# Six instead of four whole-array f-tiles at the head of block 0, taken row tile by row tile of x

## The chip, the cores and the metric

The kernel runs on one core of a Trainium2 chip. The metric is the device time of one execution in microseconds (us), lower is better. All engines of the core run side by side[...]: PE (TensorE, with its weight loads listed apart as PEld), DVE (VectorE), ACT (ScalarE), POOL (GpSimd) and SP (SyncE, which here only issues DMAs).

## What is computed

A two-layer block with a squared ReLU between the layers. x is 2048 x 576, w1 576 x 4608, w2 4608 x 576, all bf16.

```python
h = jnp.einsum("bsd,df->bsf", x, w1) + b1
r = jnp.where(h > zero, h, zero)
h = r * r
out = jnp.einsum("bsf,fd->bsd", h, w2) + b2
```

## The kernel before

**Tiles.** The 2048 rows of x are four blocks of 512 (SB); a block is four row tiles of 128 (RT). The 4608 columns of w1 are 36 f-tiles of 128 (NFT). The contraction over 576 is four chunks of 128 rows (NC) and a rest of 64. Phase A makes the transposed hidden layer hT, 128 f x 512 rows per f-tile and block; phase B (L311 to L338) multiplies it with w2.

**The usual step of phase A.** `a_step(b, j)` (L216) makes the two f-tiles of pair j with 18 matmuls of 64 contraction rows each, nine for each f-tile, in `a_part` (L208, matmul L213). One f-tile uses the upper 64 rows of the PE array and the other the lower 64, so two matmuls run side by side. Its weights lie in `w1h`, which is cut into nine pieces of 64 rows for that purpose, and it needs the transposed block xT in both halves of the partitions; `place` (L201) says where a piece lies. `evac_h` (L195) then takes each f-tile out of PSUM: ScalarE adds b1 and applies the ReLU (L197), VectorE squares (L199).

**The head of block 0.** Blocks 1 to 3 get xT by a transposing DMA (`load_xT`, L263). That would be late for block 0, so block 0 loads x as it is (`load_x`, L91), transposes it on PE into PSUM (`transpose_chunks`, L177, matmul L182) and copies the result to xT on VectorE or ScalarE (`copy_psum`, L171: L175 on VectorE, L173 on ScalarE, and L187). While `w1h` is still on its way, the first G = 4 f-tiles (two pairs) are made another way, with the whole array: `load_quad` (L94) brings 128 rows of w1 by 4 x 128 columns, and `full_mm(half, c)` (L225, matmul L228) multiplies chunk c by half a block, 256 columns at a time, into four PSUM banks bk0. The rest of 64 contraction rows is added from `qr` at L254. Three copies on VectorE (L256 to L258) then fill the second halves of xT, the four banks are evacuated (L259), and `a_step(0, 2)` to `a_step(0, 17)` follow (L292). In blocks 1 to 3 all 18 pairs go through `a_step`, those of the head last (L298).

**The order of the work.** It is written by hand: each engine runs its instructions as the program lists them. The order at the head before the change is

```python
    transpose_chunks(0, (0,), (V,))
    transpose_chunks(0, (1,), (A,))
    transpose_chunks(0, (2,), (A,))
    transpose_chunks(0, (NC,), (V,))
    full_mm(0, 0)
    transpose_chunks(0, (3,), (A,))
    full_mm(0, 1)
    full_mm(0, 2)
    transpose_chunks(1, (0, 1), (V, A))
    full_mm(0, 3)
```

and so on (L240 to L255). One half of a block is two row tiles of x, so a transposed chunk needs two of the four loads of x.

**Queues and buffers.** Eight loads are issued at the opening barrier (`issue_at_barrier`, L126, moves them there), four on SP's queue (x row tile 0, w1 chunks 0 and 2, x row tile 3) and four on ScalarE's (x row tile 1, w1 chunk 1, x row tile 2, w1 chunk 3). After the barrier SP issues the two rests (L104) and then the pieces of `w1h` (L99), pair 2 first. The DMAs use eight semaphores in turn, so that each waits for the one eight before it. Five warm-up matmuls on constant data (L169) run on PE from the barrier on. PSUM has eight banks of 128 x 512 fp32, all in one pool.

Of the kernel before, what the change touches and what calls it, by code (L numbers as in the profile page):

```python
# [11 lines left out]
BF16 = mybir.dt.bfloat16  # L12
# [5 lines left out]
def kernel(  # L18
# [9 lines left out]
    nc = tc.nc  # L28
    P = 128
    H = 64  # L30
    x2 = x.flatten_outer_dims()
    out2 = out.flatten_outer_dims()
    S, D = x2.shape
    F = w1.shape[1]
    FH = F // 2
    G = 4
    NFT = F // P
    NJ = NFT // 2
    NC = D // P
    NH = D // H  # L40
    DM = NC * P
    SB = 512
    NSB = S // SB
    RT = SB // P
    HALF = SB // 2
# [9 lines left out]
    psum = ctx.enter_context(tc.tile_pool(name="psum", bufs=8, space=PSUM))  # L55

    def bank(name):
        return psum.tile([P, SB], FP32, name=name, tag="bank")
# [10 lines left out]
    def early(n):  # L69
        at[0] += n  # L70
        assert at[0] <= NFT * D
        return w2_sb[:, at[0] - n:at[0]]


    xT = [early(XW).rearrange("p (w s) -> p w s", s=SB) for b in range(NSB - 1)]
    xT3 = xpool.tile([P, NH, SB], BF16, name="xT3", tag="xT3")
    xT.append(xT3[:])
    xs = early(RT * D).rearrange("p (j c) -> p j c", c=D)
    qn = early(NC * 4 * P).rearrange("p (c f) -> p c f", c=NC)
    qr = early(2 * P)  # L80
    pairs = [(0, 2), (1, 3)] + [(f, f + G) for f in range(G, NFT) if (f // G) % 2]
    slot = {ft: (h, j) for j, pr in enumerate(pairs) for h, ft in enumerate(pr)}
    assert len(pairs) == NJ and len(slot) == NFT

# [6 lines left out]
    def load_x(eng, j):  # L91
        eng.dma_start(out=xs[:, j, :], in_=x_view[:, j, :])

    def load_quad(eng, c):  # L94
        eng.dma_start(out=qn[:, c, :], in_=w1[c * P:(c + 1) * P, 0:G * P])

    def load_w1(eng, h, j0, n, cs):
        f0 = pairs[j0][h] * P
        eng.dma_start(out=w1h[h * H:(h + 1) * H, cs, j0 * P:(j0 + n) * P], in_=w1_rows[:, cs, f0:f0 + n * P])  # L99
# [1 line left out]
    NWARM = 5  # L101

    def load_rest(eng, h):
        eng.dma_start(out=qr[h * H:(h + 1) * H, :], in_=w1[DM:D, 2 * h * P:2 * (h + 1) * P])  # L104

    b1T = const.tile([P, NFT], FP32, name="b1T")
    warm = const.tile([P, 1], FP32, name="warm")
    load_x(nc.sync, 0)
    load_x(nc.scalar, 1)
    load_quad(nc.sync, 0)  # L110
    load_quad(nc.scalar, 1)
    load_quad(nc.sync, 2)
    load_x(nc.scalar, 2)
    load_x(nc.sync, 3)
    load_quad(nc.scalar, 3)
    nc.scalar.activation(out=warm[:], in_=nc.const_aps.tensor(1.0, [P, 1], FP32), func=ACT.Relu)
    for h in range(2):
        load_rest(nc.sync, h)


    for j0, n in ((2, 1), (3, 1), (4, 1), (5, 1), (6, 1), (7, 1), (8, 2), (10, 2), (12, 2), (14, 4)):
        for h in range(2):
            load_w1(nc.sync, h, j0, n, slice(0, NH))


    def issue_at_barrier(nc):  # L126
        entry, body = nc.main_func.blocks[:2]
        for engine in (mybir.EngineType.SP, mybir.EngineType.Activation):
            mine = [i for i in body.instructions if i.engine == engine and not isinstance(i, mybir.InstNoOp)]
            n = 0  # L130
            while isinstance(mine[n], mybir.InstDMACopy) and not mine[n].has_wait():
                n += 1
            assert n >= 3
            at = next(k for k, i in enumerate(entry.instructions)
                      if i.engine == engine and isinstance(i, mybir.InstEventSemaphore))
            for k, i in enumerate(mine[:n]):
                body.instructions.remove(i)
                entry.instructions.insert(at + k, i)

    nc.at_finalize(issue_at_barrier)  # L140


# [17 lines left out]
    ident = const.tile([P, P], BF16, name="ident")  # L160
# [10 lines left out]
    def copy_psum(eng, dst, src):  # L171
        if eng is nc.scalar:
            nc.scalar.copy(out=dst, in_=src)  # L173
        else:
            nc.vector.tensor_copy(out=dst, in_=src)  # L175

    def transpose_chunks(half, cs, engs):  # L177
        tps = [psum.tile([P, HALF], BF16, name="tp", tag="bank") for c in cs]
        for i in range(2):
            for c, tp in zip(cs, tps):  # L180
                d0 = c * P if c < NC else D - P
                nc.tensor.transpose(tp[:, i * P:(i + 1) * P], xs[:, 2 * half + i, d0:d0 + P], ident[:])  # L182
        cols = slice(half * HALF, (half + 1) * HALF)
        for c, tp, eng in zip(cs, tps, engs):
            copy_psum(eng, xT[0][:, c if c < NC else 7, cols], tp[:])
            if c == NC:
                nc.vector.tensor_copy(out=xT[0][0:H, 8, cols], in_=tp[H:P, :])  # L187

    def hT_of(b, ft):
        if b < NSB - 1:  # L190
            return hT[b][:, ft, :].rearrange("p (j s) -> p j s", j=RT)
        h, j = slot[ft]
        return w1h[:, h * RT:(h + 1) * RT, j * P:(j + 1) * P]

    def evac_h(b, ft, bk):  # L195
        r = rpool.tile([P, SB], BF16, name="r", tag="r")
        nc.scalar.activation(out=r[:], in_=bk[:], func=ACT.Relu, bias=b1T[:, ft:ft + 1], scale=1.0)  # L197
        r3 = r[:].rearrange("p (j s) -> p j s", j=RT)
        nc.vector.tensor_tensor(out=hT_of(b, ft), in0=r3, in1=r3, op=ALU.mult)  # L199

    def place(hi, c):  # L201
        if hi:
            return c // 2 if c % 2 else (3 + c // 2 if c else 8)
        return 8 if c == 8 else (4 if c % 2 else 0) + c // 2
# [11 lines left out]
    def a_step(b, j):  # L216
        bk = [bank("ph") for _ in range(2)]
        a_part(b, j, bk, range(NH))
        for h in range(2):
            evac_h(b, pairs[j][h], bk[h])  # L220


    bk0 = [bank("ph") for _ in range(G)]

    def full_mm(half, c):  # L225
        cols = slice(half * HALF, (half + 1) * HALF)
        for q in range(4):
            nc.tensor.matmul(bk0[q][:, cols], lhsT=qn[:, c, q * P:(q + 1) * P], rhs=xT[0][:, c, cols],  # L228
                             start=(half == 0 and c == 0), stop=False, skip_group_check=True)

    V, A = nc.vector, nc.scalar
    transpose_chunks(0, (0,), (V,))
    transpose_chunks(0, (1,), (A,))
    transpose_chunks(0, (2,), (A,))
    transpose_chunks(0, (NC,), (V,))
    full_mm(0, 0)
    transpose_chunks(0, (3,), (A,))
    full_mm(0, 1)
    full_mm(0, 2)
    transpose_chunks(1, (0, 1), (V, A))  # L240
    full_mm(0, 3)
    transpose_chunks(1, (2, NC), (A, V))
    full_mm(1, 0)
    transpose_chunks(1, (3,), (V,))
    full_mm(1, 1)
    b1T_ps = psum.tile([P, P], BF16, name="b1T_ps", tag="bank")
    nc.tensor.transpose(b1T_ps[:], b1_rows[:], ident[:])  # L247
    nc.vector.tensor_copy(out=b1T[:], in_=b1T_ps[:, 0:NFT])
    full_mm(1, 2)
    full_mm(1, 3)  # L250
    for i in range(2):
        for h in range(2):
            rows = slice(h * H, (h + 1) * H)
            nc.tensor.matmul(bk0[2 * h + i][:], lhsT=qr[rows, i * P:(i + 1) * P], rhs=xT[0][rows, place(h, 8), :],  # L254
                             start=False, stop=True, skip_group_check=True)  # L255
    nc.vector.tensor_copy(out=xT[0][0:H, 4:7, :], in_=xT[0][H:P, 0:3, :])  # L256
    nc.vector.tensor_copy(out=xT[0][H:P, 4:7, :], in_=xT[0][0:H, 1:4, :])
    nc.vector.tensor_copy(out=xT[0][H:P, 8, :], in_=xT[0][0:H, 0, :])  # L258
    for q in range(G):  # L259
        evac_h(0, q, bk0[q])  # L260


    def load_xT(b):  # L263
# [3 lines left out]

    load_xT(1)
    for h in range(2):
        load_w1(nc.sync, h, 0, 2, slice(0, NH))  # L270
    for b in range(2, NSB):
        load_xT(b)
    w2_view = w2_dram.rearrange("(ft p) d -> p ft d", p=P)
# [2 lines left out]
    def load_w2(c, n=1):  # L276
        nc.sync.dma_start(out=w2_sb[:, c * W2CH * D:(c + n) * W2CH * D].rearrange("p (ft d) -> p ft d", d=D),
                          in_=w2_view[:, c * W2CH:(c + n) * W2CH, :])
# [9 lines left out]
    def finish_xT(b):  # L288
        nc.vector.tensor_copy(out=xT[b][0:H, 8, :], in_=xT[b][H:P, 7, :])
        nc.vector.tensor_copy(out=xT[b][H:P, 8, :], in_=xT[b][0:H, 0, :])  # L290

    for j in range(2, NJ):  # L292
        a_step(0, j)
        if j == NJ - 2:
            finish_xT(1)
    load_w2(0)
    for b in range(1, NSB):
        for j in (*range(2, NJ), 0, 1):  # L298
            a_step(b, j)
            if j == NJ // 2 and b + 1 < NSB:  # L300
                finish_xT(b + 1)
        if b == 1:
            load_w2(1)
        if b == 2:
            load_w2(2, 2)
# [5 lines left out]
    for pr in range(NSB // 2):  # L311
        pc = bank("pc")
        for ft in range(NFT):
            for h in range(2):
                nc.tensor.matmul(pc[h * H:(h + 1) * H, :], lhsT=w2(ft, DM, D), rhs=hT_of(2 * pr + h, ft),  # L315
                                 start=(ft == 0), stop=(ft == NFT - 1))
# [52 lines left out]
```

## Time and profile before

| what | before |
|---|---|
| three runs | 289.96, 290.08, 290.81 us (median 290.08) |
| the profiled execution | 290.45 us, of it span 288.7 us |
| PE busy | 284.9 us (99%) |
| weight loads (PEld) busy | 133.7 us (46%) |
| DVE, ACT busy | 79.5 us (28%), 95.6 us (33%) |
| granted TensorE clock in the span | 1.00 |
| HBM read, written | 11.94 MB, 2.36 MB |

The span runs from the first to the last instruction of the profiled execution; 1.75 us of that execution's own time lie around it. In the profile's groups, a line gives source line, engine, operation, output and input tiles by name, shape, count, then busy time and mean ns of one, then the idle time of the engine just before, with what ended it. `w_sb` in the names stands for the large weight buffer: at the head of the kernel it holds x, xT, the chunks of w1 and their rest, since w2 arrives later. Matmuls are pipelined, so a matmul's recorded length (273 ns for 256 columns) is longer than the distance to the next one; what counts for the time is the distance. The chain of waits leads back from the last instruction, at each step to what released it; its pieces are given in order of time as start, length, what.

### The profile page before, as it was taken

Reading aid. Unit: us, or ns where it says so; the run is one execution under the profiler, and the core shown is the slowest. Engines: PE = TensorE matmul, PEld = TensorE weight load, DVE = VectorE, ACT = ScalarE, POOL = GpSimd, SP = SyncE. Lnnn points to the kernel's source line nnn. Section 1 sums busy time; section 2 is a strip of 40 time slices with the busy share of each in tenths; the row PEclk is TensorE's granted clock in tenths of the full one; section 3 lists DMA queues with packets and bytes.
Section 4 is the critical chain, followed back from the end, with each engine's and each line's share of the span. In section 5 each row is a group of like instructions: output and inputs, shape, how many; then the busy total and the mean of one; then the engine's idle time right before and its main releaser. Section 6 shows DMA issues by size and latency. Waiting matters only on the chain.

```text
span 288.7 us, 4818 instructions
## 1 busy us (share of the span) xinstructions
PE 284.9 (99%) x2067; PEld 133.7 (46%) x2078; DVE 79.5 (28%) x196; ACT 95.6 (33%) x153; POOL 1.5 (1%) x8
## 2 busy tenths in 40 slices
PE   9999999999999999999999999999999999999996
PEld 5544444444444444444445444444444444444454
DVE  1644454444445444444420011111100111111111
ACT  3666666766666676666620000000000000000000
POOL 2000000000000000000000000000000000000000
PEclk9999999999999999999999999999999999999999
DMA  7999999910400004300000100000000000000000
GB/s 200 205 190 204 172 185 208 321 50 2 122 3 0 3 2 142 106 0 2 0 2 19 20 20 20 20 23 5 15 20 23 20 20 20 23 20 22 20 23 20
DMA packets 35381, 18.01 MB, mean 62 GB/s; under 512 B 21652, under 2 KB 35360, under 8 KB 35360
## 3 DMA queue, kind: packets, MB, share of 16 engines
q1 hardware_dynamic: 34752, 17.14, 26.4%
q10 hardware_dynamic: 576, 0.56, 0.6%
q8 instruction: 16, 0.26, 0.4%
q14 instruction: 5, 0.04, 0.0%
q0 software_dynamic: 32, 0.01, 0.0%
HBM read 11.94 MB, written 2.36 MB: 50 GB/s over the span
## 4 chain that ended last, share of the span: by engine, by line
PE 98%; DMA 1%; issue 0%; DVE 0%; ACTq 0%
PE ph L213 47%; PE po L329 43%; PE pc L315 5%; PE ph L228 2%; DMA w_sb<-in_x_dram 1%; PE tp L182 1%; PE ph L254 0%; DVE o_sb L331 0%; PE b1T_ps L247 0%; ACTq L353 0%
## 5 line engine op out<-in xcount | busy, mean ns | idle before, releaser
L197 ACT ACTIVATE r<-ph,b1T 128x512 bf16<-128x512 f32 x144 | 91.0, 685 | 48.4 <-PE ph L213 46.4
L213 PE MATMUL ph<-w_sb,w1h 64*128 64x512 bf16 x936 | 101.2, 376 | 0.0
L213 PEld LDWEIGHTS <-w1h 64*128 64x128 bf16 x1260 | 61.3, 94 | 74.6
L329 PE MATMUL po<-w_sb,hT 128*128 128x512 bf16 x423 | 92.9, 379 | 0.5
L329 PEld LDWEIGHTS <-hT 128*128 128x128 bf16 x432 | 42.2, 98 | 51.2 <-issue 0.4
L199 DVE TENSOR_TENSOR hT<-r 128x512 bf16<-128x512 bf16 x108 | 46.0, 426 | 54.7 <-ACT r L197 54.2
L331 DVE TENSOR_TENSOR o_sb<-po,b_bc 128x512 bf16<-128x512 f32 (+2 forms) x17 | 11.2, 660 | 116.7 <-PE po L329 109.7
L213 PE MATMUL ph<-xT,w1h 64*128 64x512 bf16 x324 | 35.1, 376 | 0.0
L329 PE MATMUL po<-w_sb,w1h 128*128 128x512 bf16 (+2 forms) x178 | 31.2, 336 | 0.1
L329 PEld LDWEIGHTS <-w1h 128*128 128x128 bf16 x180 | 16.2, 98 | 15.3
L199 DVE TENSOR_TENSOR w1h<-r 128x512 bf16<-128x512 bf16 x36 | 15.3, 426 | 19.6 <-ACT r L197 19.5
L315 PE MATMUL pc<-hT,w_sb 128*64 128x512 bf16 x108 | 15.7, 379 | 0.0
L315 PEld LDWEIGHTS <-w_sb 128*64 128x64 bf16 x144 | 8.1, 110 | 7.6 <-issue 0.4
L315 PE MATMUL pc<-w1h,w_sb 128*64 128x512 bf16 x36 | 7.9, 379 | 0.0
L317 ACT ACTIVATE oc<-pc,b2T 128x512 bf16<-128x512 f32 x2 | 1.4, 687 | 13.7 <-PE pc L315 13.7
L325 DVE COPY o_sb<-oc 128x64 bf16<-128x64 bf16 x16 | 2.8, 172 | 9.3 <-DMA oc<-oc 9.3
L228 PE MATMUL ph<-w_sb 128*128 128x256 bf16 x32 | 5.3, 313 | 0.0
L228 PEld LDWEIGHTS <-w_sb 128*128 128x128 bf16 x32 | 3.4, 115 | 0.6
L175 DVE COPY w_sb<-tp 128x256 bf16<-128x256 bf16 x5 | 1.5, 292 | 5.9 <-PE tp L182 5.9
L182 PE MATMUL tp<-ident,w_sb 128*128 128x128 bf16 x20 | 2.7, 264 | 0.1
L169 PE MATMUL wps<-one 128*128 128x512 bf16 x5 | 2.3, 628 | 0.4 <-DVE one L144 0.4
L182 PEld LDWEIGHTS <-w_sb 128*128 128x128 bf16 x20 | 1.9, 118 | 1.4 <-DMA w_sb<-in_x_dram 1.2
(27 smaller groups left out, 10.7 us busy)
## 6 DMA issues: line engine op xcount, KB each, us to landing
w_sb<-in_w_dram SPq DMA_DIRECT2D x2, 1728.0 KB, 8.7
w1h<-in_w_dram SPq DMA_DIRECT2D x8, 288.0 KB, 5.9
out_dram<-o_sb SPq DMA_DIRECT2D x15, 144.0 KB, 1.8
w1h<-in_w_dram SPq DMA_DIRECT2D x12, 144.0 KB, 3.7
w_sb<-in_w_dram SPq DMA_DIRECT2D x2, 864.0 KB, 7.2
w1h<-in_w_dram SPq DMA_DIRECT2D x2, 576.0 KB, 11.2
w_sb<-in_x_dram SPq DMA_DIRECT2D x2, 144.0 KB, 3.4
w_sb<-in_x_dram ACTq DMA_DIRECT2D x2, 144.0 KB, 3.5
```

The source lines that it names most:

```text
L169: nc.tensor.matmul(wps[:], lhsT=ones[:, 0:P], rhs=ones[:], start=(i == 0), stop=(i == NWARM - 1))
L175: nc.vector.tensor_copy(out=dst, in_=src)
L182: nc.tensor.transpose(tp[:, i * P:(i + 1) * P], xs[:, 2 * half + i, d0:d0 + P], ident[:])
L197: nc.scalar.activation(out=r[:], in_=bk[:], func=ACT.Relu, bias=b1T[:, ft:ft + 1], scale=1.0)
L199: nc.vector.tensor_tensor(out=hT_of(b, ft), in0=r3, in1=r3, op=ALU.mult)
L213: nc.tensor.matmul(bk[h][:], lhsT=w1h[rows, c, j * P:(j + 1) * P], rhs=xT[b][rows, place(h, c), :], start=(i == 0), stop=(i == NH - 1))
L228: nc.tensor.matmul(bk0[q][:, cols], lhsT=qn[:, c, q * P:(q + 1) * P], rhs=xT[0][:, c, cols], start=(half == 0 and c == 0), stop=False, ski ...
L315: nc.tensor.matmul(pc[h * H:(h + 1) * H, :], lhsT=w2(ft, DM, D), rhs=hT_of(2 * pr + h, ft), start=(ft == 0), stop=(ft == NFT - 1))
L317: nc.scalar.activation(out=oc[:, pr, :], in_=pc[:], func=ACT.Identity, bias=b2T[:], scale=1.0)
L325: nc.vector.tensor_copy(out=o_sb[:, DM:D], in_=o_tr[pr][:, jj, h * H:(h + 1) * H])
L329: nc.tensor.matmul(po[:, 0:e - a], lhsT=hT_of(b, ft)[:, jj, :], rhs=w2(ft, a, e), start=(ft == 0), stop=(ft == NFT - 1))
L331: nc.vector.tensor_tensor(out=o_sb[:, a:e], in0=po[:, 0:e - a], in1=b2_bc[:, a:e], op=ALU.add)
```

## The change

G becomes 6, so three pairs instead of two are made with the whole array in block 0, and `a_step(0, j)` begins with j = 3. The pairs are formed anew: (0, 3), (1, 4), (2, 5), and then (6 + i, 21 + i). The loads are regrouped: all four row tiles of x on SP's queue, all four chunks of w1, now 128 x 768, on ScalarE's, all eight at the barrier. The transposes are made row tile by row tile: `transpose_tile(j, c, n, eng)` transposes n chunks of row tile j into one PSUM tile and copies them with one instruction on one engine (with two for the rest). `full_mm(j, n, c)` multiplies chunk c by n row tiles from j on, so by 128, 256 or 512 columns, for six f-tiles. The order of these calls is new. `w1h` is loaded from pair 3 on, and pairs 0 to 2 are loaded later with 384 columns at a time where 0 and 1 came with 256. The copies L256 to L258, the evacuation, phase B and the loads of w2 are as before.

```diff
     S, D = x2.shape
     F = w1.shape[1]
     FH = F // 2
-    G = 4
+    G = 6
+    GP = G // 2
     NFT = F // P
     NJ = NFT // 2
     NC = D // P
...
     xT3 = xpool.tile([P, NH, SB], BF16, name="xT3", tag="xT3")
     xT.append(xT3[:])
     xs = early(RT * D).rearrange("p (j c) -> p j c", c=D)
-    qn = early(NC * 4 * P).rearrange("p (c f) -> p c f", c=NC)
-    qr = early(2 * P)
-    pairs = [(0, 2), (1, 3)] + [(f, f + G) for f in range(G, NFT) if (f // G) % 2]
+    qn = early(NC * G * P).rearrange("p (c f) -> p c f", c=NC)
+    qr = early(GP * P)
+    pairs = [(i, GP + i) for i in range(GP)] + [(G + i, G + NJ - GP + i) for i in range(NJ - GP)]
     slot = {ft: (h, j) for j, pr in enumerate(pairs) for h, ft in enumerate(pr)}
     assert len(pairs) == NJ and len(slot) == NFT
 
...
     NWARM = 5
 
     def load_rest(eng, h):
-        eng.dma_start(out=qr[h * H:(h + 1) * H, :], in_=w1[DM:D, 2 * h * P:2 * (h + 1) * P])
+        eng.dma_start(out=qr[h * H:(h + 1) * H, :], in_=w1[DM:D, GP * h * P:GP * (h + 1) * P])
 
     b1T = const.tile([P, NFT], FP32, name="b1T")
     warm = const.tile([P, 1], FP32, name="warm")
-    load_x(nc.sync, 0)
-    load_x(nc.scalar, 1)
-    load_quad(nc.sync, 0)
-    load_quad(nc.scalar, 1)
-    load_quad(nc.sync, 2)
-    load_x(nc.scalar, 2)
-    load_x(nc.sync, 3)
-    load_quad(nc.scalar, 3)
+    for j in range(RT):
+        load_x(nc.sync, j)
+        load_quad(nc.scalar, j)
     nc.scalar.activation(out=warm[:], in_=nc.const_aps.tensor(1.0, [P, 1], FP32), func=ACT.Relu)
     for h in range(2):
         load_rest(nc.sync, h)
 
 
-    for j0, n in ((2, 1), (3, 1), (4, 1), (5, 1), (6, 1), (7, 1), (8, 2), (10, 2), (12, 2), (14, 4)):
+    for j0, n in ((3, 1), (4, 1), (5, 1), (6, 1), (7, 1), (8, 1), (9, 1), (10, 2), (12, 2), (14, 4)):
         for h in range(2):
             load_w1(nc.sync, h, j0, n, slice(0, NH))
 
...
             n = 0
             while isinstance(mine[n], mybir.InstDMACopy) and not mine[n].has_wait():
                 n += 1
-            assert n >= 3
+            assert n >= RT
             at = next(k for k, i in enumerate(entry.instructions)
                       if i.engine == engine and isinstance(i, mybir.InstEventSemaphore))
             for k, i in enumerate(mine[:n]):
...
         else:
             nc.vector.tensor_copy(out=dst, in_=src)
 
-    def transpose_chunks(half, cs, engs):
-        tps = [psum.tile([P, HALF], BF16, name="tp", tag="bank") for c in cs]
-        for i in range(2):
-            for c, tp in zip(cs, tps):
-                d0 = c * P if c < NC else D - P
-                nc.tensor.transpose(tp[:, i * P:(i + 1) * P], xs[:, 2 * half + i, d0:d0 + P], ident[:])
-        cols = slice(half * HALF, (half + 1) * HALF)
-        for c, tp, eng in zip(cs, tps, engs):
-            copy_psum(eng, xT[0][:, c if c < NC else 7, cols], tp[:])
-            if c == NC:
-                nc.vector.tensor_copy(out=xT[0][0:H, 8, cols], in_=tp[H:P, :])
+    def transpose_tile(j, c, n, eng):
+        cols = slice(j * P, (j + 1) * P)
+        tp = psum.tile([P, n, P], BF16, name="tp", tag="bank")
+        for k in range(n):
+            d0 = (c + k) * P if c < NC else D - P
+            nc.tensor.transpose(tp[:, k, :], xs[:, j, d0:d0 + P], ident[:])
+        c0 = c if c < NC else 7
+        copy_psum(eng, xT[0][:, c0:c0 + n, cols], tp[:])
+        if c == NC:
+            copy_psum(eng, xT[0][0:H, 8, cols], tp[H:P, 0, :])
 
     def hT_of(b, ft):
         if b < NSB - 1:
...
             evac_h(b, pairs[j][h], bk[h])
 
 
+    V, A = nc.vector, nc.scalar
+    transpose_tile(0, 0, 2, V)
+    transpose_tile(0, 2, 2, A)
+    transpose_tile(0, NC, 1, V)
     bk0 = [bank("ph") for _ in range(G)]
 
-    def full_mm(half, c):
-        cols = slice(half * HALF, (half + 1) * HALF)
-        for q in range(4):
+    def full_mm(j, n, c):
+        cols = slice(j * P, (j + n) * P)
+        for q in range(G):
             nc.tensor.matmul(bk0[q][:, cols], lhsT=qn[:, c, q * P:(q + 1) * P], rhs=xT[0][:, c, cols],
-                             start=(half == 0 and c == 0), stop=False, skip_group_check=True)
-
-    V, A = nc.vector, nc.scalar
-    transpose_chunks(0, (0,), (V,))
-    transpose_chunks(0, (1,), (A,))
-    transpose_chunks(0, (2,), (A,))
-    transpose_chunks(0, (NC,), (V,))
-    full_mm(0, 0)
-    transpose_chunks(0, (3,), (A,))
-    full_mm(0, 1)
-    full_mm(0, 2)
-    transpose_chunks(1, (0, 1), (V, A))
-    full_mm(0, 3)
-    transpose_chunks(1, (2, NC), (A, V))
-    full_mm(1, 0)
-    transpose_chunks(1, (3,), (V,))
-    full_mm(1, 1)
+                             start=(j == 0 and c == 0), stop=False, skip_group_check=True)
+
+    full_mm(0, 1, 0)
+    transpose_tile(1, 0, 2, V)
+    transpose_tile(1, 2, 2, A)
+    full_mm(1, 1, 0)
+    full_mm(0, 2, 1)
+    transpose_tile(1, NC, 1, V)
+    transpose_tile(2, 0, 2, A)
+    full_mm(2, 1, 0)
+    transpose_tile(2, 2, 2, V)
+    full_mm(2, 1, 1)
+    full_mm(0, 2, 2)
+    transpose_tile(2, NC, 1, A)
+    transpose_tile(3, 0, 2, V)
+    full_mm(3, 1, 0)
+    transpose_tile(3, 2, 2, A)
+    full_mm(3, 1, 1)
+    transpose_tile(3, NC, 1, V)
+    full_mm(2, 2, 2)
     b1T_ps = psum.tile([P, P], BF16, name="b1T_ps", tag="bank")
     nc.tensor.transpose(b1T_ps[:], b1_rows[:], ident[:])
     nc.vector.tensor_copy(out=b1T[:], in_=b1T_ps[:, 0:NFT])
-    full_mm(1, 2)
-    full_mm(1, 3)
-    for i in range(2):
+    full_mm(0, RT, 3)
+    for i in range(GP):
         for h in range(2):
             rows = slice(h * H, (h + 1) * H)
-            nc.tensor.matmul(bk0[2 * h + i][:], lhsT=qr[rows, i * P:(i + 1) * P], rhs=xT[0][rows, place(h, 8), :],
+            nc.tensor.matmul(bk0[GP * h + i][:], lhsT=qr[rows, i * P:(i + 1) * P], rhs=xT[0][rows, place(h, 8), :],
                              start=False, stop=True, skip_group_check=True)
     nc.vector.tensor_copy(out=xT[0][0:H, 4:7, :], in_=xT[0][H:P, 0:3, :])
     nc.vector.tensor_copy(out=xT[0][H:P, 4:7, :], in_=xT[0][0:H, 1:4, :])
     nc.vector.tensor_copy(out=xT[0][H:P, 8, :], in_=xT[0][0:H, 0, :])
-    for q in range(G):
-        evac_h(0, q, bk0[q])
+    for i in range(GP):
+        for h in range(2):
+            evac_h(0, GP * h + i, bk0[GP * h + i])
 
 
     def load_xT(b):
...
 
     load_xT(1)
     for h in range(2):
-        load_w1(nc.sync, h, 0, 2, slice(0, NH))
+        load_w1(nc.sync, h, 0, GP, slice(0, NH))
     for b in range(2, NSB):
         load_xT(b)
     w2_view = w2_dram.rearrange("(ft p) d -> p ft d", p=P)
...
         nc.vector.tensor_copy(out=xT[b][0:H, 8, :], in_=xT[b][H:P, 7, :])
         nc.vector.tensor_copy(out=xT[b][H:P, 8, :], in_=xT[b][0:H, 0, :])
 
-    for j in range(2, NJ):
+    for j in range(GP, NJ):
         a_step(0, j)
         if j == NJ - 2:
             finish_xT(1)
     load_w2(0)
     for b in range(1, NSB):
-        for j in (*range(2, NJ), 0, 1):
+        for j in (*range(GP, NJ), *range(GP)):
             a_step(b, j)
             if j == NJ // 2 and b + 1 < NSB:
                 finish_xT(b + 1)
```

## The prediction

> **What bounds the kernel now.** I read the page first: busy time by engine, then the idle time that the groups list.
>
> ```profile
> PE 284.9 (99%) x2067; PEld 133.7 (46%) x2078; DVE 79.5 (28%) x196; ACT 95.6 (33%) x153; POOL 1.5 (1%) x8
> ...
> L213 PE MATMUL ph<-w_sb,w1h 64*128 64x512 bf16 x936 | 101.2, 376 | 0.0
> ...
> L182 PEld LDWEIGHTS <-w_sb 128*128 128x128 bf16 x20 | 1.9, 118 | 1.4 <-DMA w_sb<-in_x_dram 1.2
> ```
>
> PE is the bound. The matmuls of `a_step` never wait (0.0), so no load of `w1h` is late; the wait that a DMA ends is 1.2 us, for x at the start. What is left is how fast PE gets through the head of block 0. The chain of waits gives it piece by piece (start, length, what):
>
> ```profile
> 0.21 2.84 DMA w_sb<-in_x_dram
> 3.04 0.05 issue
> 3.09 0.93 PE tp L182 x7
> 4.02 0.85 PE ph L228 x4
> 4.87 0.21 PE tp L182 x2
> 5.09 1.36 PE ph L228 x8
> 6.45 0.22 PE tp L182 x4
> 6.67 0.44 PE ph L228 x4
> ...
> 9.24 0.54 PE ph L254 x4
> 9.78 135.97 PE ph L213 x1260
> ```
>
> From 3.09 on the chain is PE alone: no copy and no load holds it up. The same work becomes cheaper on the way: four L228 of 256 columns take 0.85 us at 4.0 and 0.44 at 6.7. The timeline of the head, PE and the copies:
>
> ```profile
> 4.88 1.57 PE L228 MATMUL ph<-w_sb 128*128 128x256 bf16 x8
> ...
> 6.28 0.39 PE L182 MATMUL tp<-ident,w_sb 128*128 128x128 bf16 x4
> 6.50 0.60 PE L228 MATMUL ph<-w_sb 128*128 128x256 bf16 x4
> 6.65 0.29 DVE L175 COPY w_sb<-tp 128x256 bf16<-128x256 bf16 x1 [1.99 <-PE tp L182]
> 6.70 0.37 ACT L173 COPY w_sb<-tp 128x256 bf16<-128x256 bf16 x1 [1.21 <-PE tp L182]
> 6.94 0.39 PE L182 MATMUL tp<-ident,w_sb 128*128 128x128 bf16 x4
> ```
>
> Eight L228 from 4.88 to the next start at 6.28 are 1.40 us; at 0.213 us each before and 0.109 after, 5.1 of them were slow, so the pace changes at 4.88 + 5.1 x 0.213 = 5.96. The four transposes from 6.28 to 6.50 are 0.056 us apart, so the fourth starts at 6.45 and its ScalarE copy at 6.70, 0.25 later; the third starts at 6.39, its VectorE copy at 6.65, 0.26 later. PE does not feel this: four L228 stand between a transpose and the matmul that needs its copy.
>
> **What the skill says.** "TensorE: Matmul & The Clock Gate", Part 1, has the array at half clock until it has been busy for about 3.4 us, in a window that runs free of the kernel. The trace agrees on the factor (0.213 to 0.109). The same page, "The mechanism" in Part 3, says matmuls are a strict FIFO, and only weight loads are pulled ahead: a matmul that waits for a copy holds everything behind it. Its "Back-to-back issue gap" gives about 81 ns for 128 columns with their weight load in a long stream; the trace has 56 ns, but for four in a row. "DMA: Bandwidth & Descriptors", "Issuing engines are not separate DMA queues": regrouping by queue alters order, not bandwidth; here rows of both queues land at about the same pace (below).
>
> **The change, part by part.**
>
> *Columns of matmul.* Two f-tiles cost the same either way. `a_step` takes nine concurrent pairs: 135.97 / 1260 x 2 = 0.216 each, 1.94 us. The head takes 8 x 512 columns at 0.109 per 256, 1.74 us, and one pair for the rest, 0.22: 1.96. One `a_step` fewer and two f-tiles more at the head: zero. Transposes: 20 before and after, zero.
>
> *Weight loads.* Before, 32 L228 of 256 columns; after, six f-tiles by six of 128, three of 256 and one of 512 columns: 60. About 24 of the 128-column ones run at full clock. Low bound 0.056 each (nothing extra), high bound the page's 81 ns, 24 x 0.025 = 0.6 us. I take 0, because the four transposes have a full weight load each at that pace.
>
> *The loads.* All land in time, I think. Landing is issue plus these times (x row tile 0 issued at 0.09 and 1 at 0.21; x row tile 3 at 1.47 and chunk 3 at 1.58):
>
> ```profile
> w_sb<-in_x_dram SPq DMA_DIRECT2D x1, 144.0 KB, 2.6
> w_sb<-in_x_dram ACTq DMA_DIRECT2D x1, 144.0 KB, 2.8
> ...
> w_sb<-in_x_dram SPq DMA_DIRECT2D x1, 144.0 KB, 4.3
> w_sb<-in_w_dram ACTq DMA_DIRECT2D x1, 128.0 KB, 4.3
> ```
>
> So 2.7, 3.0, 5.8, 5.9. After, 1344 KB instead of 1088; at about 375 GB/s (the bins from 2 to 3 us) the last one comes 0.7 us later, about 6.6. Estimates from the order: x0 2.7, chunk 0 3.3, x1 3.7, chunk 1 4.2, x2 5.2, chunk 2 6.0, x3 6.2, chunk 3 6.6 to 7.1. Below, each is needed later than that, by 0.2 us (chunk 0) to over 4 us (chunk 3). The rests move behind four x tiles and are needed at 12.5. `w1h` of pair 3 is issued like pair 2 before, at 4.3, and needed 3.5 us later than that one. Some pieces of `w1h` now wait for later loads (eight semaphores in turn: x2, chunk 2, x3, chunk 3), about 0.5 us, against a stream that makes a pair every 1.5 us where PE takes 1.94. The transposed loads of block 1 stay 3 us and more ahead. POOL's work is not passed by anything. Cost of all this: 0; if chunk 0 came 0.5 us later than estimated, 0.25.
>
> *The waits.* This is where time goes. Wherever the matmul after a row tile's transposes needs their copy at once, PE stops. The gap, from the second transpose of a pair: 0.26 to the copy, 0.29 (VectorE) or 0.37 (ScalarE) for it, about 0.05 for the semaphore (0.03 from L197 to L199 and 0.07 from L144 to L169 are what the timeline shows), less what PE issues meanwhile. Worked through at 0.107 us per 128 columns until 5.95 and 0.055 after:
>
> - 2.70 to 3.24 five transposes of x0 (before, one, and then the wait for x1). Copy 3.15 to 3.44, `full_mm(0,1,0)` from 3.49 (idle 0.25) to 4.13.
> - Four transposes of x1 to 4.56; VectorE copy 4.59 to 4.88; `full_mm(1,1,0)` 4.93 (idle 0.37) to 5.57. `full_mm(0,2,1)` to 6.41.
> - Three transposes to 6.58. `full_mm(2,1,0)` needs a ScalarE copy: 6.52 + 0.26 + 0.37 + 0.05 = 7.20, idle **0.62**, then to 7.53. Two transposes, `full_mm(2,1,1)`, `full_mm(0,2,2)` to 8.62 without a wait.
> - Three transposes to 8.79. `full_mm(3,1,0)` needs a VectorE copy: 8.73 + 0.60 = 9.33, idle **0.54**, to 9.66. Two transposes and `full_mm(3,1,1)` to 10.10, one transpose to 10.16.
> - `full_mm(2,2,2)` needs the ScalarE copy of 9.71: 10.39, idle **0.23**, to 11.05. Bias transpose, `full_mm(0,4,3)` 1.30: 12.40. As before, 0.1 to the rests, and 0.22 per pair of them, 0.65: `a_step(0,3)` starts at 13.15.
>
> Before, `a_step(0,2)` starts at 9.62 (timeline), `a_step(0,3)` 1.94 later: 11.56. Difference **+1.6 us**: 1.4 from the three bold gaps, 0.2 from the two early ones, which count half because they lie in slow time. What sat behind the waits, all of PE's queue, shifts with them; nothing later has slack to give it back, as PE is 99% busy.
>
> *Behind the head.* Six evacuations instead of four: L197 takes about 0.6 each, 3.6 us. With eight banks, `a_step(0,3)` takes two free ones and `a_step(0,4)`, 1.94 later, the first two evacuated. ScalarE needs 1.4 per step afterwards. Cost 0. The copies L256 to L258 (1.4 us) lie beside 2.6 us of matmuls, more cover than before.
>
> The sum stands against the profiled execution, 290.45 (span 288.7 and 1.75 around it); that is 0.37 above the median. Carried to the median: 290.08 + 1.6 = **291.7**. A measurement here tells about 0.3%, 0.87 us, from no change.
>
> **The rivals.**
>
> - *The clock is released a window later.* Between 2.5 and 5.95 PE idles 0.6 us after the change and 0.3 before; if that keeps the array slow for another 3.4 us, then `full_mm(0,2,1)` to `full_mm(2,1,1)` run at half pace and `full_mm(0,2,2)` ends at 10.0 instead of 8.62: +1.4 more, **293.1**. For it: 2.1 us of warm-up matmuls from 0.38 on released nothing. Against: PE is still busy over 80% of that time.
> - *Small matmuls are bound by weight loads.* +0.6, **292.3**. Against: the 56 ns above.
> - *Not slower.* The window runs free and PE's dense work begins at 2.70, not 3.09. If the clock is released earlier in the runs after, all slow pieces shrink. With release at 2.70 the first copy is done at 3.31 and `full_mm(2,1,0)` ends at 6.44 instead of 7.53: +0.5, **290.6**. By a line between the two (+1.6 at 5.95, +0.5 at 2.70) it decides from about 3.8 on: released before that, the difference is under 0.87. For it: the runs before spread by 0.85. Against: the same warm-up on both sides.
> - *A load comes late* (chunk 0 or x1): under +0.4, inside the range.
>
> **How the numbers follow.** Forecast as worked 0.60 (own range 291.2 to 292.2); later release 0.14; weight loads 0.10; not slower 0.12; a gain from something I do not see 0.04, since the whole head has only the 0.39 us between 2.70 and 3.09 to win. Slower by over 0.3%: 0.60 + 0.14 + 0.10 = 0.84; within 0.12; faster 0.04. The range, 290.8 to 293.2, leaves out most of the last two.
>
> **What would show it.** In the profile after: PE idle 0.5 to 0.6 us twice between 6.4 and 9.4 and about 0.2 near 10.2, each ended by a copy; pace change near 5.95; 0.056 between the 128-column L228; no PE wait on a DMA but the first; L213 starting at about 13.15, and 0.0 idle in it. Wrong if the gaps are absent or end with a DMA, or if L213 starts before 12.4.

## The result, and the profile after

The changed kernel takes 291.76 us (median of 4 runs, 291.52 to 291.99), the kernel before 290.02 beside it (4 runs, 289.95 to 290.81). The ratio is 1.0054, with a 95% interval of 1.0033 to 1.0074: slower by 1.0 to 2.1 us, as forecast (291.7).

The page of the changed kernel, busy time and the groups that answer to those shown of before (`a_step`'s matmul is now L208, `full_mm`'s L227, the transposes L178):

```profile
PE 285.2 (98%) x2078; PEld 134.3 (46%) x2090; DVE 79.8 (28%) x199; ACT 95.5 (33%) x154; POOL 1.5 (1%) x8
...
L208 PE MATMUL ph<-w_sb,w1h 64*128 64x512 bf16 x918 | 99.2, 376 | 0.0
...
L227 PE MATMUL ph<-w_sb 128*128 128x128 bf16 (+2 forms) x59 | 6.9, 269 | 1.2 <-DVE w_sb L171 0.6
...
L227 PEld LDWEIGHTS <-w_sb 128*128 128x128 bf16 x60 | 5.2, 107 | 2.5 <-issue 1.8
```

The group of before that answers to L227:

```profile
L228 PE MATMUL ph<-w_sb 128*128 128x256 bf16 x32 | 5.3, 313 | 0.0
```

`a_step` waits as little as before (0.0). New is the idle time ahead of L227, 1.2 us, ended by the copies out of PSUM; before, L228 had 0.0. The timeline shows where, in start, length, engine, line and count, with the idle time before it and what ended that in brackets:

```profile
2.75 0.71 PE L178 MATMUL tp<-ident,w_sb 128*128 128x128 bf16 x5
...
3.52 0.80 PE L227 MATMUL ph<-w_sb 128*128 128x128 bf16 x6
...
4.12 0.63 PE L178 MATMUL tp<-ident,w_sb 128*128 128x128 bf16 x4
...
4.92 1.54 PE L227 MATMUL ph<-w_sb 128*128 128x128 bf16 x12 [0.17 <-DVE w_sb L171]
...
6.30 0.33 PE L178 MATMUL tp<-ident,w_sb 128*128 128x128 bf16 x3
...
6.67 0.37 ACT L169 COPY w_sb<-tp 128x256 bf16<-128x256 bf16 x1 [1.51 <-PE tp L178]
7.09 0.49 PE L227 MATMUL ph<-w_sb 128*128 128x128 bf16 x6 [0.46 <-ACT w_sb L169]
...
8.53 0.33 PE L178 MATMUL tp<-ident,w_sb 128*128 128x128 bf16 x3
...
8.89 0.29 DVE L171 COPY w_sb<-tp 128x256 bf16<-128x256 bf16 x1 [0.87 <-PE tp L178]
9.24 0.49 PE L227 MATMUL ph<-w_sb 128*128 128x128 bf16 x6 [0.38 <-DVE w_sb L171]
...
9.88 0.37 ACT L169 COPY w_sb<-tp 128x256 bf16<-128x256 bf16 x1 [0.56 <-PE tp L178]
...
10.02 0.22 PE L178 MATMUL tp<-ident,w_sb 128*128 128x128 bf16 x1
...
10.30 0.82 PE L227 MATMUL ph<-w_sb 128*128 128x256 bf16 x6
...
13.06 2.11 PE L208 MATMUL ph<-w_sb,w1h 64*128 64x512 bf16 x18
```

In this stretch PE issues a transpose every 0.056 us, so it is done issuing at 6.30 + 3 x 0.056 = 6.47 and goes on at 7.09: 0.62 us lost. Likewise 8.69 to 9.24 (0.54, rounded from finer times) and 10.07 to 10.30 (0.23). The brackets show less (0.46, 0.38, nothing), because a transpose's record lasts 0.22 us, longer than the distance to the next; a gap between issues has to be taken from starts. At the slow pace of the first microseconds (0.107 us per 128 columns) two more gaps stand, 0.27 us ahead of 3.52 and 0.38 ahead of 4.92. `a_step(0,3)` starts at 13.06. Before, `a_step(0,2)` started at 9.62 and the next step 1.94 later, at 11.56. The difference, 1.50, is that of the two spans (290.2 and 288.7): nothing was lost or won behind the head. The other traces say the same: from the first matmul of `a_step` to the last matmul of the kernel it is 274.15 us in every kernel with six f-tiles and 276.10 in every one with four, which has one step of 1.94 more. Up to the last matmul, the head alone decides.

The chain of waits of the changed kernel would mislead here:

```profile
7.91 3.30 DMA w1h<-in_w_dram
11.21 0.02 issue
11.23 1.24 PE ph L227 x5
12.47 0.76 PE ph L255 x6
```

It names a load of `w1h` as what released PE at 11.23. But of the six L227 with 512 columns, which take chunk 3, only five were recorded (x59 in the page where the kernel has 60, while PEld has all 60). They are 0.216 apart, and the first recorded one starts at 11.23; the bias transpose before them starts at 10.96 and takes 0.056. A sixth matmul at 11.01 fills the place exactly. PE did not wait there.

### The profile page after: what moved, and what is told of

It is laid out like the page before. It is cut to its first block, busy times and chain, and to the rows that moved or that the text cites. A ratio compares the mean times of both kernels' runs of the same rounds, so it can differ in the third digit from the quotient of the medians.

```text
span 290.2 us, 4844 instructions
## 1 busy us (share of the span) xinstructions
PE 285.2 (98%) x2078; PEld 134.3 (46%) x2090; DVE 79.8 (28%) x199; ACT 95.5 (33%) x154; POOL 1.5 (1%) x8
## 4 chain that ended last, share of the span: by engine, by line
PE 95%; DMA 2%; SPq 2%; issue 0%; DVE 0%; ACTq 0%
PE ph L208 46%; PE po L331 43%; PE pc L317 5%; DMA w1h<-in_w_dram 1%; SPq L100 1%; DMA w_sb<-in_w_dram 1%; PE ph L227 0%; SPq L105 0%; PE ph L255 0%; DVE o_sb L333 0%; ACTq L355 0%
## 5 line engine op out<-in xcount | busy, mean ns | idle before, releaser
L208 PE MATMUL ph<-w_sb,w1h 64*128 64x512 bf16 x918 | 99.2, 376 | 0.0
L208 PEld LDWEIGHTS <-w1h 64*128 64x128 bf16 x1242 | 60.4, 94 | 73.6
L208 PE MATMUL ph<-xT,w1h 64*128 64x512 bf16 x324 | 35.1, 376 | 0.0
L227 PE MATMUL ph<-w_sb 128*128 128x128 bf16 (+2 forms) x59 | 6.9, 269 | 1.2 <-DVE w_sb L171 0.6
L227 PEld LDWEIGHTS <-w_sb 128*128 128x128 bf16 x60 | 5.2, 107 | 2.5 <-issue 1.8
L171 DVE COPY w_sb<-tp 128x256 bf16<-128x256 bf16 (+2 forms) x10 | 2.5, 251 | 7.9 <-PE tp L178 7.8
L169 ACT COPY w_sb<-tp 128x256 bf16<-128x256 bf16 (+2 forms) x6 | 2.0, 334 | 4.7 <-PE tp L178 4.7
L178 PE MATMUL tp<-ident,w_sb 128*128 128x128 bf16 x20 | 2.8, 260 | 0.1
```

The lines of the kernel that those rows point to most:

```text
L178: nc.tensor.transpose(tp[:, k, :], xs[:, j, d0:d0 + P], ident[:])
L208: nc.tensor.matmul(bk[h][:], lhsT=w1h[rows, c, j * P:(j + 1) * P], rhs=xT[b][rows, place(h, c), :], start=(i == 0), stop=(i == NH - 1))
```

## The experiments

Six runs, each timed beside the kernel before (290.2, and 290.3 for the last two).

**1. The waits covered.** The changed kernel with only the order and the widths of the calls at the head made anew. Ahead of the part shown, `full_mm(0, 1, 1)` now stands before `full_mm(1, 1, 0)`; after it, chunks 2 and 3 of the last row tiles are taken in calls of 128 columns. The middle:

```diff
-    full_mm(0, 2, 1)
     transpose_tile(1, NC, 1, V)
     transpose_tile(2, 0, 2, A)
+    full_mm(1, 1, 1)
+    full_mm(0, 2, 2)
+    transpose_tile(2, 2, 2, V)
     full_mm(2, 1, 0)
-    transpose_tile(2, 2, 2, V)
     full_mm(2, 1, 1)
-    full_mm(0, 2, 2)
     transpose_tile(2, NC, 1, A)
     transpose_tile(3, 0, 2, V)
+    full_mm(2, 1, 2)
+    full_mm(0, 2, 3)
+    transpose_tile(3, 2, 2, A)
     full_mm(3, 1, 0)
```

> The changed kernel with its calls at the head in another order: the transposes of a row tile are issued one or two full_mm ahead of the matmul that needs their copy, and chunks 1 to 3 are taken in smaller pieces to fill (12 calls of 128 columns and two of 256 instead of six, three and one). Loads, six f-tiles, copies and engines as in the changed kernel. Theory (PE waits for the copies): the gaps measured in the changed kernel's trace, 0.62, 0.54 and 0.23 us at full clock and 0.37 at half clock, go; 1.40 + 0.19 less than the 291.8 of the changed kernel, so about 290.1 to 290.3, no different from before. Rival (small matmuls cost more through their weight loads): 72 instead of 36 matmuls of 128 columns, so no gain or up to 0.9 us more, 291.8 to 292.7. Rival (six f-tiles or the loads cost the time): unchanged, 291.8.

Measured: 290.42 us, ratio to before 1.0006 (0.9994 to 1.0017). Its group of L227 in the groups by line:

```profile
L227 PE MATMUL ph<-w_sb 128*128 128x128 bf16 (+1 forms) x84 | 6.6, 232 | 0.1
```

The idle time is down from 1.2 to 0.1, and the time is that of before as far as the interval tells, 0.1 above what was expected. Loads, f-tiles, copies and their engines are those of the changed kernel, so none of them is what makes it slower. There are twice as many matmuls of 128 columns (72), so they are not dear either; the end of the head in the chain of waits has 34 instructions of 128 columns in a row, bias transpose and row tile transposes among them (the pieces of this chain go by the ends of the records):

```profile
8.44 0.11 PE tp L178 x2
8.55 0.67 PE ph L227 x12
9.22 0.06 PE tp L178
9.28 0.67 PE ph L227 x12
9.95 0.06 PE b1T_ps L253
10.00 0.34 PE ph L227 x6
```

That is 1.90 us from 8.44 to 10.34, 0.056 each.

One load came late in this execution: row tile 1 of x landed at 4.13 us where in the changed kernel's trace it landed at 3.6, and its transposes at 4.18 started 0.24 us after the matmuls ahead of them had been issued. One of the 22 runs took 293.17 us.

**2. Four f-tiles, row tile by row tile.** The changed kernel with the order and the queues kept:

```diff
-    G = 6
+    G = 4
...
-    for j0, n in ((3, 1), (4, 1), (5, 1), (6, 1), (7, 1), (8, 1), (9, 1), (10, 2), (12, 2), (14, 4)):
+    for j0, n in ((2, 1), (3, 1), (4, 1), (5, 1), (6, 1), (7, 1), (8, 1), (9, 1), (10, 2), (12, 2), (14, 4)):
```

> The changed kernel with four f-tiles instead of six: row tile by row tile and the new queues stay, the chunks of w1 are 512 columns wide again. Theory (PE waits for the copies): the gaps stay, the early ones at 0.37 and 0.62 and 0.54 as they are, the last one grows from 0.23 to about 0.35 because the six matmuls that covered part of it are four; worked through in the same way a_step(0,2) starts at 11.3 us where before it starts at 9.6, so 291.5 to 291.8. Rival (six f-tiles at the head are what costs): back to 290.0.

Measured: 291.78 us, ratio 1.0051 (1.0037 to 1.0065). As slow as the changed kernel, without the six f-tiles: neither they nor the two more PSUM banks that they hold make the waits. In the timeline of PE the same two gaps at full pace stand, and the third has grown:

```profile
5.32 0.33 PE L178 MATMUL tp<-ident,w_sb 128*128 128x128 bf16 x3
6.11 0.38 PE L227 MATMUL ph<-w_sb 128*128 128x128 bf16 x4 [0.46 <-ACT w_sb L169]
...
7.11 0.33 PE L178 MATMUL tp<-ident,w_sb 128*128 128x128 bf16 x3
7.82 0.38 PE L227 MATMUL ph<-w_sb 128*128 128x128 bf16 x4 [0.38 <-DVE w_sb L171]
...
8.37 0.22 PE L178 MATMUL tp<-ident,w_sb 128*128 128x128 bf16 x1
8.77 0.60 PE L227 MATMUL ph<-w_sb 128*128 128x256 bf16 x4 [0.18 <-ACT w_sb L169]
```

From 5.32 + 0.17 to 6.11 is 0.62, from 7.11 + 0.17 to 7.82 is 0.54, from 8.37 + 0.06 to 8.77 is 0.34 (0.35 expected). `a_step(0,2)` starts at 10.66, earlier than the 11.3 expected: in this execution the pace of PE changed at about 4.75 and not at 5.95, which is worth 0.6 us (see the last section).

**3. Six f-tiles by halves of the block.** The kernel before with G = 6 and what follows from it (pairs, widths of the loads, banks taken after the first four transposes), its order and queues kept:

```diff
-    G = 4
+    G = 6
+    GP = G // 2
...
+    bk0 = [bank("ph") for _ in range(G)]
     full_mm(0, 0)
     transpose_chunks(0, (3,), (A,))
```

> The kernel before with six f-tiles instead of four and nothing else: transposes and full_mm by halves of the block in the old order, x and w1 alternating between the queues as before, chunks of w1 768 columns wide. Theory (PE waits for the copies): six matmuls of 256 columns stand between a transpose and its use, PE does not wait, two f-tiles move from a_step to the head at equal cost; 290.0 to 290.3, a_step(0,3) at about 11.6 us. Rival (six f-tiles cost, through larger loads, six evacuations or PSUM banks): 291 or more.

Measured: 290.24 us, ratio 1.0008 (0.9997 to 1.0019); `a_step(0,3)` starts at 11.70. In the median, six f-tiles at the head cost nothing that can be measured, and bring nothing; two of the 22 runs took 291.42 and 292.37 us. The timeline shows why PE does not wait in this order:

```profile
7.06 0.39 PE L183 MATMUL tp<-ident,w_sb 128*128 128x128 bf16 x4
...
7.28 0.82 PE L227 MATMUL ph<-w_sb 128*128 128x256 bf16 x6
7.43 0.29 DVE L176 COPY w_sb<-tp 128x256 bf16<-128x256 bf16 x1 [3.00 <-PE tp L183]
7.48 0.37 ACT L174 COPY w_sb<-tp 128x256 bf16<-128x256 bf16 x1 [1.78 <-PE tp L183]
...
7.94 0.39 PE L183 MATMUL tp<-ident,w_sb 128*128 128x128 bf16 x4
```

Both copies are over at 7.85, while PE works on a chunk that was copied earlier until 7.94.

**4. The loads alone.** The kernel before with the regrouped queues:

```diff
-    load_x(nc.sync, 0)
-    load_x(nc.scalar, 1)
-    load_quad(nc.sync, 0)
-    load_quad(nc.scalar, 1)
...
+    for j in range(RT):
+        load_x(nc.sync, j)
+        load_quad(nc.scalar, j)
```

> The kernel before with the loads regrouped and nothing else: the four row tiles of x on SP's queue, the four chunks of w1 on ScalarE's. Theory: the second row tile of x lands at about 3.5 us instead of 3.0, and the first transposes by halves need two row tiles, so PE starts 0.45 us later in slow time, worth about 0.2: 290.2 to 290.3. Rival (the regrouped queues cost the 1.7 us): 291 or more.

Measured: 290.89 us, ratio 1.0021 (1.0007 to 1.0034), so 0.2 to 1.0 us slower. The 0.2 expected is the lower end of that, and the median, 0.7, is well above it; the rival's 1.7 us is outside. The start:

```profile
2.74 0.29 PE L177 MATMUL tp<-ident,w_sb 128*128 128x128 bf16 x1
...
3.49 0.93 PE L177 MATMUL tp<-ident,w_sb 128*128 128x128 bf16 x7 [0.46 <-DMA w_sb<-in_x_dram]
```

The second row tile of x lands 0.4 us later than before, and a half needs both. That is worth 0.2 in slow time. `a_step(0,2)` starts 0.58 later than before (10.20); in this execution the pace changed at about 6.7 instead of 5.95, which is worth the other 0.4. Whether the pause delayed that change or chance did stays open, and so does what the other runs lost beyond 0.2; three of the 22 took 291.96 to 292.98 us. In the changed kernel the pause does not arise, as its first five transposes need row tile 0 alone, and experiment 1, with the same regrouped loads, is level with before.

**5. The three copies twice.** The changed kernel, each copy that PE waits for at full pace repeated on the same data:

```diff
-    transpose_tile(2, 0, 2, A)
+    transpose_tile(2, 0, 2, A, 2)
...
-    transpose_tile(3, 0, 2, V)
+    transpose_tile(3, 0, 2, V, 2)
...
-    transpose_tile(3, 2, 2, A)
+    transpose_tile(3, 2, 2, A, 2)
```

> The changed kernel with the three copies that PE waits for at full clock made twice over, the second on top of the first with the same data (row tile 2 chunks 0 and 1 on ScalarE, row tile 3 chunks 0 and 1 on VectorE, row tile 3 chunks 2 and 3 on ScalarE). Theory (PE waits for these copies): the three gaps of 0.62, 0.54 and 0.23 us grow by one copy each, 0.37 + 0.29 + 0.37, so 1.0 us more than the changed kernel, 292.8. Rival (the copies are beside the path, and the time goes elsewhere at the head): no change, 291.8.

Measured: 293.12 us, ratio 1.0094 (1.0079 to 1.0108): 1.36 us more than the changed kernel's 291.76, which was not timed beside it; by the two ratios it is 0.40% of 290.2, 1.2 us. The first gap in the timeline:

```profile
6.56 0.33 PE L178 MATMUL tp<-ident,w_sb 128*128 128x128 bf16 x3
...
6.93 0.78 ACT L169 COPY w_sb<-tp 128x256 bf16<-128x256 bf16 x2 [2.17 <-PE tp L178]
...
7.75 0.49 PE L228 MATMUL ph<-w_sb 128*128 128x128 bf16 x6 [0.86 <-ACT w_sb L169]
```

It is 1.03 us (6.73 to 7.75) instead of 0.62, 0.04 more than one ScalarE copy of 0.37: the second copy starts that much after the first. The other two are 0.87 and 0.64, so the three grew by 1.13 in all (from finer times), 0.10 above the forecast. Of the eight profiled executions this is the only one in which a chunk of w1 came late:

```profile
5.89 0.83 PE L228 MATMUL ph<-w_sb 128*128 128x256 bf16 x6 [0.78 <-DMA w_sb<-in_w_dram]
```

That is chunk 1, which landed at 5.85 here and at 4.15 in the changed kernel's trace.

**6. Six warm-up matmuls.** Experiment 1 with `NWARM = 6` for 5.

> The kernel with the covered order and six f-tiles, with six warm-up matmuls instead of five, so that PE has no pause between them and the first transpose. The sixth ends at about 2.9 us and pushes the first transposes back by 0.2 us in slow time, 0.1 in the sum. Theory (the moment at which PE gets to full pace, between 4.6 and 6.6 us in the profiles so far, does not depend on what the kernel does): 290.3 to 290.5, no different from five. Rival (it depends on PE being busy without a pause from the barrier on): the moment comes by 4.6 us in nearly every run, 289.7 to 289.9, and the runs lie closer together.

Measured: 290.17 us (289.80 to 291.16, 14 runs), ratio 0.9998 (0.9988 to 1.0008). That is not different from before, and 0.1 below what the theory gave. The rival's 289.7 to 289.9 lies below the interval, which in us is 290.0 to 290.5; the runs do not lie closer together than those of before (289.58 to 290.82); and in the profiled execution, with no pause between warm-up and transposes, the pace changed at about 5.0 and not by 4.6. So the rival falls, if not by much. No order of the head tried here beats the kernel before.

## Why the prediction was right

- *The waits.* Forecast gaps 0.62, 0.54 and 0.23; the trace has 0.62, 0.54 and 0.23. The two early ones were 0.27 and 0.38 against 0.25 and 0.37. That a waiting matmul holds what stands behind it shows in experiment 2: the transposes next in line had their data since 4.61 and start at 6.33, behind the matmuls that waited until 6.11. Experiment 1 takes the three late waits and the second early one away, but for 0.1 us, and the time goes with them; experiment 5 lengthens the three and it follows. For these three this is shown, and not only argued. The first early wait stays in experiment 1 (0.27 us ahead of the matmul at 3.34), and what the second cost was not tried by itself.
- *The sum.* +1.6 was forecast; the trace gives 1.50, the timed runs 1.74 (1.0 to 2.1). `a_step(0,3)` was put at 13.15 and starts at 13.06; most of that 0.09 is the pace, which changed at 5.8 and not at 5.95.
- *Columns and six f-tiles at zero.* Right: experiment 3 leaves the time as it is, within -0.1 to 0.6 us.
- *Weight loads at zero.* Right: experiment 1 runs 34 in a row, with a weight load each, 0.056 apart. The 81 ns that the Trainium skill gives for a long stream ("TensorE: Matmul & The Clock Gate", "Back-to-back issue gap") do not show here; the measurement decides.
- *Loads in time.* Right for the changed kernel: PE waits for a DMA once, for the first row tile at 2.75. Row tile 1 landed at 3.6 (3.7 estimated). But the late chunk 1 of experiment 5 shows that the margin I counted for it (needed at 5.57, estimated at 4.2) can be used up, and row tile 1 came late in the trace of experiment 1. The rival has a place, then, and did not show in the profile of the result. It may be behind the single long runs of experiments 1, 3 and 4, up to 2.8 us above their medians, where 78 runs of the kernel before never passed 290.85; none of those runs was profiled, so this is not shown.
- *The clock.* The rival of a later release did not come: in the changed kernel six L227 of 256 columns go from 5.51 to 6.30, 0.79 us = 1.3 x 0.213 + 4.7 x 0.109, so the pace changed at about 5.8. That I set 5.95 for both sides was luck; one execution of either could have had another value.
- *Behind the head.* Right: with six evacuations L208 still has 0.0 idle.
- *Not slower.* Fell: all four runs lie between 291.52 and 291.99, and in the profiled one the pace changed at 5.8, not before the 3.8 that the rival needed. What it built on is real, though: in the trace of experiment 5 the pace changed before 3.3 (last section).

## What to carry to other kernels

Between producing something on one engine and using it after a second engine's copy, count the whole latency (here 0.26 + 0.37 + 0.05 us) against the work that stands between them in the program's order; splitting work into smaller tiles in the old order of use shrinks that cover even when it shrinks nothing else, and in experiment 1 an order with more work between copy and use gave it back. Before moving work to the head of a bound engine, see whether it idles there: here it had 0.39 us to win, and a reorder that takes work in row by row put 1.4 us of waits in. When an execution's chain of waits names a load, check that the matmuls behind it were all recorded.

## What the runs showed of the hardware

The granted clock in the profile reads 1.00 also where PE runs at the slow pace (before, 2 to 4 us); the pace can be read only from the distance between starts. The moment at which PE gets to full pace differs from execution to execution much more than I had assumed. At 0.107 us per 128 columns before it and 0.056 after, it is before 3.3 us in the trace of experiment 5, before 4.3 in that of 1, about 4.75 in 2, 5.0 in 6, 5.8 in the changed kernel, 5.95 in the kernel before, 6.4 in 3 and 6.7 in 4. (The 4.6 to 6.6 in the expectation of experiment 6 was too narrow.) Each microsecond of slow pace costs PE about half a microsecond of work at the head, so the 3.4 us between the ends are worth up to 1.7, an estimate. The kernel before alone spreads over 1.3 us (289.58 to 290.85); that this is the reason is likely, but was not tried by itself. Nothing in these eight traces ties the moment to what the kernel does. The Trainium skill's "TensorE: Matmul & The Clock Gate", Part 1, says that the window runs free and that the start of full pace varies between runs; it puts the variation at half a microsecond in one place, and the traces have over three.
